# A local-attention and PReLU feed-forward kernel: the list that orders its first stage is rewritten, with maxima subtracted on VectorE and low parts formed in PSUM

## The chip, the cores and the metric

One core of one Trainium2 chip. The metric is device time in microseconds (us) of one execution; three executions of the kernel before took 771.10, 771.13 and 771.49 us, median 771.13.

## The reference, cut to what matters

```python
# q, k, v: (8, 8, 576, 64); sequence cut into chunks of 64; scale = 1/8
scores = scale * np.matmul(q_c, k_c.transpose(0, 1, 2, 4, 3))   # within a chunk
scores = scores - np.max(scores, axis=-1, keepdims=True)
attn = np.exp(scores)
attn = attn / (np.sum(attn, axis=-1, keepdims=True) + 1e-09)
out = np.matmul(attn, v_c)
x = out laid out as (4608 tokens, 512)
h = x @ w_in                                   # 512 x 2048
g = np.maximum(h, 0.0) + alpha * np.minimum(h, 0.0)
return g @ w_out                               # 2048 x 512
```

The weights arrive as 64-bit floats. The kernel turns each weight chunk into a 32-bit value and splits that into a high part and a low part in the matmul's input format; activations are split the same way, and each large product is made of three passes (high by high, low by high, high by low).

## The kernel before, in words

**Tiling.** The 4608 tokens are 36 sub-blocks of 128 tokens (two attention chunks each); four sub-blocks make a block of 512 tokens. The feed-forward's 2048 inner columns are 16 chunks `f` of 128. A first-layer step `h<b><f>` (line 422) is 12 matmuls of 128x512, an output step `o<b><f>` (line 458) is 12 more, into four PSUM tiles `t` of 128 tokens (two in the pair `ps_oa`, two in `ps_ob`). The first stage does the attention of sub-blocks 0 to 7, chunks 0 to 2 of block 0 and chunks 0 to 7 of block 1, and prepares weight chunks 0 to 8 of both matrices. Behind it come the rest of blocks 0 and 1, block 2, and pairs of blocks with a Strassen-like scheme whose weights are stored to DRAM by `keep_a` (line 597) and read back.

**What orders the first stage.** The string `START` (line 28) lists tokens; a loop (lines 931 to 932) issues them, and the order that results on PE, DVE, ACT, POOL and SP is kept as it stands. Each engine works through its own instructions in order. The tokens are:

- `q`, `k`, `v`: a load on SP's DMA queue (`q0`, `q1` on ACT's), lines 548 and 555; from 2 on, one load holds two sub-blocks. `W<n>`: n products of a zero tile, nothing reads them (line 898).
- `S<s>`: the 16 score products (line 261), into a PSUM bank pair. `m`: the row maxima, DVE (line 298). `z`, `e`, `a`, `r`, `n`: softmax (lines 299 to 325). For a sub-block in `SUBTRACTED`, `z` subtracts the maxima on DVE (302), `e` is one exponential on ACT (304), `a` a sum and an addition on DVE (307, 317). For the others, `z` scales the maxima on DVE (309), `e` is eight exponentials with accumulated sums, read straight from PSUM (313), `a` an addition on POOL (319). `r` is the reciprocal (321), `n` the multiplication (323), both on DVE.
- `T`: four transposes on PE (349). `p`: their copy to SBUF on ACT (356). `V`: 16 value products (367). `x`: the high part of x on ACT (373). `l`: the low part on DVE (375).
- `wi<f>`, `wo<f>` without a letter: the fetch of a raw weight chunk, 512 KB, on SP's queue (178). With a letter, the steps of its conversion: `b` absolute value on ACT (194), `k`, `h`, `u`, `v` bit work on DVE (196 to 202), `i` the high part on ACT (207), `j` the low part on DVE (209). `wi0` does `b` and `i` on DVE.
- `h`, `R`, `G`, `gh`, `gl`, `o`: the first layer on PE, its negative part on ACT (407), the PReLU on DVE (410), the high part on ACT (436), the low part on DVE (439), the output product on PE. `K<t>`: an output tile of block 0 is copied by ACT (492) and stored by a DMA on SP's queue (495).

**Buffers that make waits.** `BANKS` gives each S, T and V its PSUM pair: 0 is `ps_a`, 1 and 2 are `ps_oa` and `ps_ob`, which the output steps need from `o00` on. The tile `g` has two buffers, so `R` of one chunk waits for `gl` of the chunk two before. A `ps_h` bank (two of them) is free again after `G`. The 18 raw chunks of the list go round ten buffers (lines 169 to 177), so from the eleventh fetch on each waits for the conversion step `v` of the fetch ten before. `HALVES` names the scratch tile (`ta`, `tb`, `tc`) of each conversion. Outside the list, `keep_a` is issued by POOL once the last sub-block's low part is there (line 953) and the chunk is converted. Behind the list come `h18`, `o17` and, in an order that the framework's planner chooses, the next steps.

Of the kernel before, what the change touches and what calls it, by code (L numbers as in the profile page):

```python
# [10 lines left out]
F32 = mybir.dt.float32  # L11
# [8 lines left out]
def bits(pattern):  # L20
# [8 lines left out]
W8 q0 k0 k1 q1 q2 S0 W1 k2 m0 S1 W5 wi1 z0 m1 e0 wi0 z1 a0 e1 r0 S2 k4 n0 S3 m2 q4 wi1b z2 T0 W6 m3  # L29
e2 a1 z3 wi1k v0 wi0b r1 wi1h n1 wi2 p0 wi0k T1 a2 e3 wi0h r2 S4 W3 v2 wi0u n2 m4 q6 p1 V0 a3 z4  # L30
wi0v e4 T2 W4 k6 r3 wi0i wi1u wi0j wo4 wi1v x0 V1 n3 p2 wo0 l0 x1 V2 wi2b a4 l1 T3 x2 wo1 wi2k S5 p3
l2 wi1i V3 m5 v6 S6 r4 x3 z5 n4 e5 wi4 l3 h00 m6 v4 wi2h z6 wi1j e6 wi2u S7 wi3 a5 wi2v h01 m7 wo2
r5 R00 z7 n5 wo0b G00 wi5 wi2i T5 e7 wo0k wi2j h02 wi7 a6 wo0h r6 wo0u wo5 n6 p5 wo0v gh00 T6 wo1b
a7 T4 wo3 gl00 wo0i V5 r7 wo1k p6 wo0j x5 V6 n7 p4 l5 x6 T7 wo1h V4 l6 p7 wo1u x4 o00 R01 wo1v wo2b
G01 wo1i l4 gh01 wo1j R02 V7 gl01 o01 x7 wo2k G02 wi4b wi3b wo2h wo2u gh02 l7 h10 wo2v gl02 wo2i
wi3k wo2j wi4k wo4b o02 wi3h wi4h R10 wo4k wi4u K0 wi3u K1 G10 h11 wi4v gh10 wi3v wi4i gl10 K2 wi3i
wo4h wi4j K3 o10 wo4u wo5b wi3j R11 wo4v wi5b G11 wo4i wo6 h12 wo5k gh11 wo4j wi6 gl11 wo3b wo5h
wo3k wo5u wo8 o11 R12 wo3h wo5v wi8 G12 wo5i wo3u gh12 wo7 h13 wo5j gl12 wi7b wo3v wi5k wo3i wi7k
wi5h o12 R13 wo3j wi5u G13 wi5v gh13 h14 wi7h wi5i gl13 wi6b wi5j wi6k wi7u wi6h o13 R14 wi7v G14
wi7i wi6u gh14 wo6b wi6v h15 gl14 wi6i wo6k wi6j wi7j wo7b wo6h o14 wo7k R15 wo6u G15 wo6v gh15 wo7h  # L40
wi8b gl15 h16 wo6i wo7u wo7v wo6j wo7i wi8k o15 wo7j R16 wo8b G16 wi8h gh16 wi8u gl16 h17 wi8v wo8k
wi8i wi8j wo8h o16 R17 G17 wo8u gh17 wo8v gl17 wo8i wo8j
# [17 lines left out]
def tile_local_attention_prelu_ffn(  # L60
# [50 lines left out]
    def f32(t):  # L111
        return t.bitcast(F32)
# [181 lines left out]
    def early_softmax(s, sc3):  # L294

        mx = small.tile([P, H, 1], F32, name="mx", bufs=2)
# [3 lines left out]
        if s in SUBTRACTED:  # L300
# [59 lines left out]
    def early_values(s):  # L360
# [720 lines left out]
```

## Time and profile before

| what | value |
|---|---|
| median of three executions | 771.13 us (771.10 to 771.49) |
| span of the profiled execution | 770.2 us; no other time of that execution is given |
| PE, DVE, ACT, POOL busy | 760.4, 646.7, 447.3, 184.8 us |
| chain that ended last | PE 92%, ACT 4%, DVE 2%, DMA 2% |
| DMA | 184.5 MB, mean 240 GB/s |

The span runs from the first to the last instruction of the program in one profiled execution; the timed executions have a median 0.9 us above it. A busy share tells how much of the span an engine had something in work, not that it set the pace. The chain of waits is followed back from the last instruction, at each step to what released it. The timeline gives the start and the duration of each instruction (like ones in a row merged, xN), with the idle time of its engine ahead of it and who ended that; durations include the pipeline's tail, so start to start is often about 0.1 us shorter.

### The profile page before, as it was taken

What the parts mean: (1) busy time and instruction counts of PE and PEld (TensorE: products, weight loads), DVE (VectorE), ACT (ScalarE), POOL (GpSimd) and SP (SyncE); (2) the same over time, 40 slices, a digit from 0 to 9 for tenths busy, and PEclk for the clock granted to TensorE, in tenths of its full rate; (3) what the DMA queues carried; (4) which work ended last, traced back from release to release, by engine and by line L of the source; (5) the groups of instructions that cost most, each with busy time, mean ns of one, the idle gap of its engine ahead of it and who ended that gap; (6) DMA issues with size and microseconds to landing.
All of it is one profiled execution on the core that took longest, in us unless ns stands there. A gap on an engine that the chain in (4) does not pass through costs nothing.

```text
span 770.2 us, 15415 instructions
## 1 busy us (share of the span) xinstructions
PE 760.4 (99%) x5558; PEld 639.8 (83%) x5558; DVE 646.7 (84%) x1140; ACT 447.3 (58%) x1221; POOL 184.8 (24%) x304
## 2 busy tenths in 40 slices
PE   7999999999999999999999999999999999999998
PEld 7788887888888888888888888888888888888886
DVE  6999988989899886877899898777898977679784
ACT  6975555576666665666657456664574544354643
POOL 1153322343254331111121121111221121122110
PEclk9999999999999999999999999999999999999999
DMA  9859496468798775878765678875656765555573
GB/s 349 337 196 386 176 324 216 163 229 226 234 238 274 240 258 200 304 275 277 263 234 197 233 250 288 269 239 206 207 193 223 260 228 193 204 205 192 198 258 144
DMA packets 69322, 184.52 MB, mean 240 GB/s; under 512 B 10992, under 2 KB 18176, under 8 KB 69120
## 3 DMA queue, kind: packets, MB, share of 16 engines
q0 software_dynamic: 34336, 119.56, 45.9%
q1 hardware_dynamic: 34480, 63.20, 24.2%
q8 instruction: 44, 0.72, 0.4%
q10 hardware_dynamic: 432, 0.79, 0.3%
q14 instruction: 30, 0.25, 0.1%
HBM read 135.27 MB, written 42.99 MB: 231 GB/s over the span
## 4 chain that ended last, share of the span: by engine, by line
PE 92%; ACT 4%; DVE 2%; DMA 2%; issue 0%; ACTq 0%; SPq 0%
PE ps_o L722 20%; PE ps_o L850 19%; PE ps_h L422 14%; PE ps_h L722 10%; PE ps_h L850 10%; PE ps_oa L458 8%; PE ps_ob L458 7%; PE ps_a L388 2%; PE ps_a L272 2%; ACT wi L313 1%; ACT wo L313 1%; DMA raw<-w_in 1%; DMA raw<-w_out 1%; PE ps_h L898 1%; ACT wi L207 0%
## 5 line engine op out<-in xcount | busy, mean ns | idle before, releaser
L422 PE MATMUL ps_h<-xh,wi 128*128 128x512 f32 x384 | 101.7, 385 | 0.7 <-DVE g L410 0.5
L422 PEld LDWEIGHTS ps_h<-xh,wi 128*128 128x128 f32 x384 | 70.7, 187 | 13.8 <-DVE g L410 0.9
L722 PE MATMUL ps_o<-wi,raw 128*128 128x512 f32 x336 | 79.1, 382 | 0.0
L722 PEld LDWEIGHTS ps_o<-wi,raw 128*128 128x128 f32 x336 | 62.5, 187 | 11.2
L678 ACT CAST gh<-wo 128x512 fp32r<-128x512 f32 x66 | 41.0, 620 | 47.4 <-PE ps_o L850 31.8
L287 ACT ACTIVATE pr<-ps_a,mx 128x64 f32<-128x64 f32 x224 | 67.2, 325 | 0.8
L458 PE MATMUL ps_oa<-wo,gh 128*128 128x512 f32 x192 | 58.5, 385 | 0.1
L458 PE MATMUL ps_ob<-wo,gh 128*128 128x512 f32 x192 | 57.7, 380 | 0.0
L422 PE MATMUL ps_h<-xl,wi 128*128 128x512 f32 x192 | 50.6, 381 | 0.0
L679 DVE TENSOR_TENSOR gl<-wo,gh 128x512 fp32r<-128x512 f32 x63 | 43.2, 686 | 7.5 <-ACT gh L678 7.1
L287 ACT ACTIVATION_READ_ACCUMULATOR pr<-ps_a,mx 128x1 f32 x224 | 48.6, 217 | 0.0
L659 POOL DMA_DIRECT2D raw<-wi_a x42 | 22.3, 531 | 102.1 <-PE ps_o L722 54.5
L659 POOL DMA_DIRECT2D raw<-wo_a x42 | 22.2, 529 | 90.8 <-PE ps_o L850 51.2
L407 ACT ACTIVATE wo<-gh 128x512 f32<-128x512 f32 x24 | 15.2, 632 | 48.5 <-DVE gh L752 48.5
L678 ACT CAST ta<-wo 128x512 fp32r<-128x512 f32 x42 | 26.1, 621 | 26.4 <-PE ps_o L850 15.2
L422 PEld LDWEIGHTS ps_h<-xl,wi 128*128 128x128 f32 x192 | 35.8, 187 | 6.7 <-DVE xl L375 0.2
L458 PEld LDWEIGHTS ps_ob<-wo,gh 128*128 128x128 f32 x192 | 35.9, 187 | 6.4
L458 PEld LDWEIGHTS ps_oa<-wo,gh 128*128 128x128 f32 x192 | 35.3, 187 | 7.0 <-ACT gh L436 0.5
L722 PE MATMUL ps_o<-wi,wo 128*128 128x512 f32 x168 | 40.4, 383 | 0.0
L722 PE MATMUL ps_o<-wi,wi 128*128 128x512 f32 x168 | 40.4, 383 | 0.0
L722 PE MATMUL ps_h<-wi,raw 128*128 128x512 f32 x168 | 40.4, 382 | 0.0
L407 ACT ACTIVATE g<-ps_h 128x512 f32<-128x512 f32 x48 | 29.5, 614 | 17.5 <-PE ps_h L422 17.5
(296 smaller groups left out, 2036.2 us busy)
## 6 DMA issues: line engine op xcount, KB each, us to landing
raw<-wi_a POOLq DMA_DIRECT2D x42, 512.0 KB, 4.4
raw<-wo_a POOLq DMA_DIRECT2D x42, 512.0 KB, 3.5
wi<-wi_a POOLq DMA_DIRECT2D x21, 512.0 KB, 3.7
wo<-wi_a POOLq DMA_DIRECT2D x21, 512.0 KB, 4.3
wi<-wo_a POOLq DMA_DIRECT2D x21, 512.0 KB, 3.5
wo<-wo_a POOLq DMA_DIRECT2D x21, 512.0 KB, 3.6
k_sb<-kT SPq DMA_DIRECT2D x28, 256.0 KB, 4.7
q_sb<-qT SPq DMA_DIRECT2D x28, 256.0 KB, 4.1
```

Source lines behind the costliest of these rows:

```text
L272: pe(nc.tensor.matmul(att[0][c * C:(c + 1) * C, par, (NP + hp) * C:(NP + hp + 1) * C], lhsT=q_sb[rows, 2 * hp + c], rhs=kb[rows, 2 * hp + ...
L287: last = nc.scalar.activation(pr[:, g], sc3[:, g // NP, g % NP], AF.Exp, bias=mx[:, g], scale=SCALE, accum_out=sm[:, g])
L313: last = nc.scalar.activation(pr[:, g], sc3[:, g % 2, g // 2], AF.Exp, bias=mx[:, g], scale=SCALE, accum_out=sm[:, g])
L388: pe(nc.tensor.matmul(att[0][par * C:(par + 1) * C, c, hp * C:(hp + 1) * C], lhsT=v_sb[rows, h * C:(h + 1) * C], rhs=p[rows, :, par * NP + ...
L407: nc.scalar.activation(g, h, AF.Relu, scale=-1.0)
L422: pe(nc.tensor.matmul(woven(hps), lhsT=wi[f][:, l, k * P:(k + 1) * P], rhs=woven(xx[:, k]), start=(i == 0 and k == 0), stop=(i == 2 and k ...
L458: pe(nc.tensor.matmul(woven(o), lhsT=a[:, ts], rhs=woven(wo[f][:, l]), start=(f == first and i == 0), stop=(f == last and i == 2),))
L659: streamed[0] = nc.gpsimd.dma_start(out=f32(t), in_=units[side][n])
L678: hi = nc.scalar.copy(t_hi, t)
L679: return hi, nc.vector.tensor_tensor(t_lo, t, f32(t_hi), op=ALU.subtract)
L722: pe(nc.tensor.matmul(woven(ps), lhsT=w[:, l, k * P:(k + 1) * P], rhs=woven(xx[:, xl]), start=first and at == 0, stop=at == n - 1, skip_gr ...
L850: pe(nc.tensor.matmul(woven(ps[m]), lhsT=w[:, l, m * P:(m + 1) * P], rhs=woven(xx), start=i in (1, 5, 2) and j == 0 and n == 0, stop=j == ...
```

## The change

Sub-blocks 2 and 4 join sub-block 0 in subtracting the maxima on VectorE. For sub-blocks 1, 2 and 3 the low part of x is formed in PSUM: a new token `X` multiplies the high part by a negative identity (`minus`, made once on ACT) and adds it to the value products in their bank (two products of 128x256), and `l` is then a copy on ACT. The six runs of zero products (27 in all) go, and one of two, `W2`, comes ahead of `S2`. PSUM is given out by bank: a pair is one tile for the whole stage, transposes take one bank of a pair or a `ps_h` bank. `mx` and `sm` get a third buffer each. The list, the scratch names and the banks are rewritten.

```diff
@@ -26,32 +26,33 @@
 
 
 START = """
-W8 q0 k0 k1 q1 q2 S0 W1 k2 m0 S1 W5 wi1 z0 m1 e0 wi0 z1 a0 e1 r0 S2 k4 n0 S3 m2 q4 wi1b z2 T0 W6 m3
-e2 a1 z3 wi1k v0 wi0b r1 wi1h n1 wi2 p0 wi0k T1 a2 e3 wi0h r2 S4 W3 v2 wi0u n2 m4 q6 p1 V0 a3 z4
-wi0v e4 T2 W4 k6 r3 wi0i wi1u wi0j wo4 wi1v x0 V1 n3 p2 wo0 l0 x1 V2 wi2b a4 l1 T3 x2 wo1 wi2k S5 p3
-l2 wi1i V3 m5 v6 S6 r4 x3 z5 n4 e5 wi4 l3 h00 m6 v4 wi2h z6 wi1j e6 wi2u S7 wi3 a5 wi2v h01 m7 wo2
-r5 R00 z7 n5 wo0b G00 wi5 wi2i T5 e7 wo0k wi2j h02 wi7 a6 wo0h r6 wo0u wo5 n6 p5 wo0v gh00 T6 wo1b
-a7 T4 wo3 gl00 wo0i V5 r7 wo1k p6 wo0j x5 V6 n7 p4 l5 x6 T7 wo1h V4 l6 p7 wo1u x4 o00 R01 wo1v wo2b
-G01 wo1i l4 gh01 wo1j R02 V7 gl01 o01 x7 wo2k G02 wi4b wi3b wo2h wo2u gh02 l7 h10 wo2v gl02 wo2i
-wi3k wo2j wi4k wo4b o02 wi3h wi4h R10 wo4k wi4u K0 wi3u K1 G10 h11 wi4v gh10 wi3v wi4i gl10 K2 wi3i
-wo4h wi4j K3 o10 wo4u wo5b wi3j R11 wo4v wi5b G11 wo4i wo6 h12 wo5k gh11 wo4j wi6 gl11 wo3b wo5h
-wo3k wo5u wo8 o11 R12 wo3h wo5v wi8 G12 wo5i wo3u gh12 wo7 h13 wo5j gl12 wi7b wo3v wi5k wo3i wi7k
-wi5h o12 R13 wo3j wi5u G13 wi5v gh13 h14 wi7h wi5i gl13 wi6b wi5j wi6k wi7u wi6h o13 R14 wi7v G14
-wi7i wi6u gh14 wo6b wi6v h15 gl14 wi6i wo6k wi6j wi7j wo7b wo6h o14 wo7k R15 wo6u G15 wo6v gh15 wo7h
-wi8b gl15 h16 wo6i wo7u wo7v wo6j wo7i wi8k o15 wo7j R16 wo8b G16 wi8h gh16 wi8u gl16 h17 wi8v wo8k
-wi8i wi8j wo8h o16 R17 G17 wo8u gh17 wo8v gl17 wo8i wo8j
+k0 q0 q1 k1 S0 k2 S1 m0 z0 e0 W2 q2 wi1 m1 z1 a0 S2 r0 e1 wi0
+S3 n0 k4 m2 q4 a1 m3 T0 wi1b z2 r1 z3 v0 n1 v2 p0 e2 T1 a2 wi2
+wi0b S5 r2 wi0k e3 p1 a3 n2 T2 wi1k m5 r3 wo0 z5 wi1h S4 m4 wi0h p2 e5
+V0 z4 a5 V2 n3 wi0u T3 x0 q6 x2 k6 r5 p3 wi2b wi0v V1 x1 e4 l0 wo2
+n5 wi0i V3 X1 X2 x3 wi1u wi3 l1 wi0j X3 T5 l2 wi1v wi5 S6 l3 a4 S7 m6
+wo0b r4 v4 wo3 wi1i z6 p5 wi1j m7 wi2k n4 e6 a6 h00 h01 z7 wi6 wi2h wo0k T4
+r6 e7 wi2u n6 a7 wi2v wo0h T6 R00 r7 V5 p4 n7 wi2i G00 x5 wo0u wo2b v6 gh00
+wi2j V4 T7 x4 wo0v p6 wo0i l4 l5 h02 p7 V6 x6 wo0j gl00 wo1 wo1b V7 wi4 l6
+wo2k o00 wo1k wo7 R01 x7 G01 R02 gh01 l7 h10 wo1h wo2h wo1u G02 wo1v wo1i wo2u gh02 wo2v
+wo1j wi3b gl01 gl02 wi4b h11 wi4k wo2i wi3k wo2j wi4h R10 o01 G10 wi6b wi6k o02 wi4u gh10 wi3h
+gl10 wi3u K2 wi6h K0 wi3v K1 wi3i wi6u wo8 wi4v wi7 R11 G11 wi6v K3 wo4 wi4i wi6i wi3j
+wi4j h12 wi5b R12 wi6j wi5k G12 o10 wo3b h13 gh11 wi5h wo3k wi5u gh12 wo6 gl12 wo3h gl11 R13
+wo4b wi5v wo4k G13 wi5i h14 wo3u wo4h wi5j o11 wo3v R14 o12 wo4u wo4v wo6b h15 gh13 wo6k wo5
+wo4i wo3i G14 wo4j wi7b gl13 wo3j wo6h gh14 wi7k wo6u wo5b wo5k wo6v wo5h wi7h wo5u gl14 wo5v o13
+wo5i wi7u wi7v wo6i R15 wi7i wo6j h16 wo8b G15 o14 wo5j wi8 gh15 wi7j R16 h17 wo8k wo7b wi8b
+G16 wo8h gl15 gh16 wo7k wi8k wo8u wi8h wo7h gl16 R17 wo8v wo7u wi8u wo7v G17 wo8i wo7i o15 wi8v
+gh17 wo7j wi8i o16 gl17 wi8j wo8j
 """
 
 ALONE = ('wi0',)
-SUBTRACTED = (0,)
+SUBTRACTED = (0, 2, 4,)
+REMAINDERS = (1, 2, 3,)
 HALVES = {
-    "wi1": "ta", "wi0": "tb", "wi2": "tc", "wo0": "tb", "wo1": "ta", "wo2": "tc", "wi4": "tb", "wi3": "ta",
-    "wo4": "tc", "wo5": "tb", "wi5": "ta", "wo3": "tc", "wi7": "tb", "wi6": "tc", "wo6": "ta", "wo7": "tc",
-    "wi8": "tb", "wo8": "ta",
+    "wi0": "tb", "wi1": "ta", "wi2": "tc", "wi3": "tb", "wi4": "tc", "wi5": "tb", "wi6": "ta", "wi7": "ta", "wi8": "ta", "wo0": "tb", "wo1": "tc", "wo2": "ta", "wo3": "tc", "wo4": "ta", "wo5": "tc", "wo6": "tb", "wo7": "tc", "wo8": "tb",
 }
 BANKS = {
-    "S0": 1, "S1": 2, "S2": 0, "S3": 1, "T0": 2, "T1": 0, "S4": 2, "V0": 1, "T2": 0, "V1": 2, "V2": 0, "T3": 1,
-    "S5": 2, "V3": 1, "S6": 0, "S7": 1, "T5": 2, "T6": 1, "T4": 2, "V5": 0, "V6": 1, "T7": 2, "V4": 0, "V7": 0,
+    "S0": 4, "S1": 2, "S2": 4, "S3": 0, "S4": 0, "S5": 2, "S6": 2, "S7": 0, "T0": 2, "T1": 4, "T2": 7, "T3": 6, "T4": 4, "T5": 7, "T6": 0, "T7": 1, "V0": 4, "V1": 2, "V2": 0, "V3": 4, "V4": 4, "V5": 2, "V6": 4, "V7": 0,
 }
 LISTED = 18
 
@@ -147,10 +148,12 @@
     nc.vector.memset(table, 0.0)
     nc.scalar.activation(table, table, AF.Exp)
 
-    small.tile([P, 24], F32, name="rest")
+    small.tile([P, 8], F32, name="rest")
     gap.tile([P, 2 * SHIFT], F32, name="between")
     ident = small.tile([P, P], F32, name="ident")
     make_identity(nc, ident)
+    minus = room(FREE + RAWS + 1, [P, P], F32R)
+    nc.scalar.mul(minus, ident, -1.0)
     alpha_sb = small.tile([P, NF], F32, name="alpha_sb")
     rise = small.tile([P, NF], F32, name="rise")
 
@@ -240,9 +243,16 @@
             loads.append(nc.sync.dma_start(out=v_sb, in_=v[:, s]))
             qkv[s][2] = v_sb
 
+    pairs = {}
+
     def banks_of(token):
-        pool, name = ((ps_a, "ps_a"), (ps_o, "ps_oa"), (ps_o, "ps_ob"))[BANKS[token]]
-        return pool.tile([P, 2, TB], F32, name=name)
+        pair, bank = divmod(BANKS[token], 2)
+        if pair == 3:
+            return ps_h.tile([P, TB], F32, name="ps_h")
+        if pair not in pairs:
+            pool, name = ((ps_a, "ps_a"), (ps_o, "ps_oa"), (ps_o, "ps_ob"))[pair]
+            pairs[pair] = pool.tile([P, 2, TB], F32, name=name)
+        return pairs[pair][:, bank] if token[0] == "T" else pairs[pair]
 
     def quads():
         for hp in range(NP):
@@ -278,9 +288,9 @@
         return att[0][:, :, NP * C:].rearrange("p b (g k) -> p b g k", k=C)
 
     def attn_softmax(s, sc3):
-        mx = small.tile([P, H, 1], F32, name="mx", bufs=2)
+        mx = small.tile([P, H, 1], F32, name="mx", bufs=3)
         pr = soft.tile([P, H, C], F32, name="pr")
-        sm = small.tile([P, H, 1], F32, name="sm", bufs=2)
+        sm = small.tile([P, H, 1], F32, name="sm", bufs=3)
         scaled = nc.vector.tensor_reduce(mx.rearrange("p (b g) k -> p b (g k)", b=2), sc3, axis=AX.X, op=ALU.max)
         nc.scalar.mul(mx, mx, -SCALE)
         for g in range(H):
@@ -293,7 +303,7 @@
 
     def early_softmax(s, sc3):
 
-        mx = small.tile([P, H, 1], F32, name="mx", bufs=2)
+        mx = small.tile([P, H, 1], F32, name="mx", bufs=3)
         pr = prs[s // 2 % 2][:, s % 2]
         nc.vector.tensor_reduce(mx.rearrange("p (g c) k -> p c (g k)", c=2), sc3, axis=AX.X, op=ALU.max)
         yield
@@ -303,12 +313,12 @@
             yield
             last = nc.scalar.activation(pr, pr, AF.Exp, scale=SCALE)
             yield
-            sm = small.tile([P, H, 1], F32, name="sm", bufs=2)
+            sm = small.tile([P, H, 1], F32, name="sm", bufs=3)
             nc.vector.tensor_reduce(sm, pr, axis=AX.X, op=ALU.add)
         else:
             scaled = nc.vector.tensor_scalar(mx, mx, -SCALE, None, op0=ALU.mult)
             yield
-            sm = small.tile([P, H, 1], F32, name="sm", bufs=2)
+            sm = small.tile([P, H, 1], F32, name="sm", bufs=3)
             for g in range(H):
                 last = nc.scalar.activation(pr[:, g], sc3[:, g % 2, g // 2], AF.Exp, bias=mx[:, g], scale=SCALE, accum_out=sm[:, g])
             yield
@@ -344,7 +354,7 @@
     def early_transpose(s):
 
         pr = probs.pop(s)
-        tp = banks_of(f"T{s}")[:, 0]
+        tp = banks_of(f"T{s}")
         for hp in range(NP):
             pe(nc.tensor.transpose(
                 tp[:, hp * P:(hp + 1) * P],
@@ -365,14 +375,21 @@
         for hp, c, par, rows, to, cols in quads():
             h = 2 * hp + par
             pe(nc.tensor.matmul(
-                xo[to, c, cols], lhsT=v_sb[rows, h * C:(h + 1) * C], rhs=p[rows, h * C:(h + 1) * C], start=True, stop=True,
+                xo[to, c, cols], lhsT=v_sb[rows, h * C:(h + 1) * C], rhs=p[rows, h * C:(h + 1) * C],
+                start=hp == 0 or s not in REMAINDERS, stop=True, skip_group_check=hp > 0,
             ))
         yield
-        xo = by_chunk(xo)
+        banks, xo = xo, by_chunk(xo)
         xh, xl = (tokens(t, s) for t in x[s // SPB])
         nc.scalar.copy(xh, xo)
         yield
-        nc.vector.tensor_tensor(xl, xo, f32(xh), op=ALU.subtract)
+        if s in REMAINDERS:
+            for c in range(2):
+                pe(nc.tensor.matmul(banks[:, c, :NP * C], lhsT=minus, rhs=xh[:, c], start=False, stop=True, skip_group_check=True))
+            yield
+            nc.scalar.copy(xl, xo)
+        else:
+            nc.vector.tensor_tensor(xl, xo, f32(xh), op=ALU.subtract)
         yield
 
     def tokens(t, s):
@@ -908,7 +925,7 @@
         elif name == "V":
             running["values", s] = early_values(s)
             next(running["values", s])
-        elif name in ("x", "l"):
+        elif name in ("x", "X", "l"):
             next(running["values", s])
         elif name == "K":
             store(accs[0], 0, True, (s,))
```

## Rows read from the trace of the kernel before

**Rows 1.** The page: busy us of the engines (share of the span), instructions
```profile
PE 760.4 (99%) x5558; PEld 639.8 (83%) x5558; DVE 646.7 (84%) x1140; ACT 447.3 (58%) x1221; POOL 184.8 (24%) x304
```

**Rows 2.** Busy time by stretch: PE, PEld, DVE, ACT, POOL; clock; DMA share, GB/s
```profile
10.00:15.00 5.00, 2.73 (x28) 2.22 (x20) 4.77 (x14) 5.00 (x31) 0.64 (x2) 1.00 1.00 378
...
35.00:40.00 5.00, 4.40 (x94) 3.52 (x87) 4.97 (x9) 4.67 (x10) 0.00 (x0) 1.00 0.07 27
...
75.00:80.00 5.00, 5.00 (x25) 4.24 (x24) 4.97 (x10) 3.64 (x7) 2.02 (x4) 1.00 0.91 316
```

**Rows 3.** Chain that ended last, 0 to 85 us: start, us, what
```profile
44.22 2.64 PE ps_h L422 x12
46.86 1.32 PE ps_oa L458 x6
48.18 1.32 PE ps_ob L458 x6
...
81.18 2.64 PE ps_h L422 x12
```

**Rows 4.** Timeline, PE alone: start, us, instructions [idle before, ended by]
```profile
1.06 3.78 PE L898 MATMUL ps_h<-wo 128*128 128x128 f32 x16 [1.06 <-DVE table L147]
...
4.77 1.13 PE L261 MATMUL ps_oa<-wo,wo 64*64 64x64 f32 x32
...
8.95 0.69 PE L261 MATMUL ps_a<-wi,wi 64*64 64x64 f32 x32
...
11.64 1.50 PE L898 MATMUL ps_h<-wo 128*128 128x128 f32 x12
...
15.06 0.69 PE L261 MATMUL ps_ob<-wo,wo 64*64 64x64 f32 x32 [0.34 <-DMA wo<-qT]
...
20.72 0.69 PE L367 MATMUL ps_a<-wi,wi 64*64 64x64 f32 x32 [0.27 <-ACT wi L356]
21.34 0.66 PE L349 MATMUL ps_oa<-ident,wi 128*128 128x128 f32 x4
...
24.14 1.15 PE L422 MATMUL ps_h<-xh,wi 128*128 128x512 f32 x4 [0.24 <-ACT xh L373]
...
86.30 1.04 PE L422 MATMUL ps_h<-xh,wi 128*128 128x512 f32 x4
```

**Rows 5.** Groups by line, 0 to 90 us: xcount | busy us, mean ns
```profile
L898 PE MATMUL ps_h<-wo 128*128 128x128 f32 x54 | 9.5, 333 | 1.1 <-DVE table L147 1.1
L375 DVE TENSOR_TENSOR xl<-ps_a,xh 128x512 fp32r<-128x512 f32 x4 | 2.7, 685 | 0.0
L302 DVE TENSOR_TENSOR wo<-ps_oa,mx 128x512 f32<-128x512 f32 x1 | 0.7, 692 | 0.0
```

**Rows 6.** Timeline, ACT: the eight exponentials of sub-block 1 and what follows; two casts
```profile
8.60 0.31 ACT L313 ACTIVATE wo<-ps_ob,mx 128x64 f32<-128x64 f32 x1 [0.55 <-DVE mx L309]
...
10.93 0.71 ACT L194 ACTIVATE ta<-raw 128x512 f32<-128x512 f32 x1
...
20.52 0.63 ACT L373 CAST xh<-ps_ob 128x512 fp32r<-128x512 f32 x1
21.00 0.73 ACT L194 ACTIVATE tc<-more 128x512 f32<-128x512 f32 x1
```

**Rows 7.** Timeline, DMA issues: SP's partial stores and fetches, POOL's `keep_a`
```profile
48.83 0.33 SPq L495 DMA_DIRECT2D partial<-wo x1
...
52.88 2.89 POOL L597 DMA_DIRECT2D wi_a<-wi x4 [1.53 <-DVE wi L209]
```

**Rows 8.** DMA queues 53 to 64 us (packets, MB, share); issues at 48.83 and 57.60 (us to landing)
```profile
q0 software_dynamic: 591, 1.92, 54.2%
q1 hardware_dynamic: 685, 2.00, 46.8%
...
partial<-wo SPq DMA_DIRECT2D x1, 256.0 KB, 3.6
...
wo<-w_in SPq DMA_DIRECT2D x1, 512.0 KB, 9.8
```

## The prediction

> **What bounds the kernel now.** PE is busy 99% of the span [rows 1], so only what shortens or delays PE's own sequence can move the end. Next I read the stretches. From 10 to 15 us PE works 2.73 of 5 us while the DMA engines are full; from 75 to 80 it works all of it, and so does DVE, nearly (4.97) [rows 2]. The chain of waits says where PE becomes solid: from 44.22 us it is PE alone, 2.64 us for a first-layer step and 1.32 + 1.32 for an output step, up to `h17` at 81.18 [rows 3]. PE's timeline gives the marks: the first scores at 4.77, `S4` at 15.06 (it waits for the load of q), `h00` at 24.14, and `h18`, the first step behind the list, at 86.30 [rows 4]. So the change is worth what it does to that 86.30, plus what DVE owes at that point, since DVE is as full as PE and has no reserve to catch up with.
>
> The profiled execution has a span of 770.2 us; the median of the runs is 0.9 above it. I take that as constant and put my shifts on the median, 771.13. About 0.2% (1.5 us) is what a measurement of this kernel can tell from no change.
>
> **The parts on ACT, DVE and POOL.** Sub-blocks 2 and 4: eight exponentials hold ACT from 8.60 to 10.93, 2.33 us [rows 6]; one exponential holds it as long as a cast, 0.48 from start to start [rows 6]. ACT gains 2 x 1.85 = 3.7 us. DVE pays a subtraction and a sum for each, 0.69 apiece as line 302 [rows 5], so 2 x 1.38 = 2.8; the small additions moved from POOL replace the small scalings, zero net. Low parts of 1, 2 and 3: DVE gives back 3 x 0.685 = 2.05 [rows 5], ACT pays 3 x 0.48 = 1.4, PE pays six products of 256 columns at half of the 0.22 that a product of 512 takes (2.64 / 12, [rows 3]), some 0.7. Net: ACT -2.3, DVE +0.7, PE +0.7. The making of `minus`, third buffers, scratch names: nothing; ACT is idle until the first exponential. (If `minus` stood ahead of the issue of q1, `S1` would come 1.4 us later; the wait of `S4` for its load would swallow that.)
>
> **The zero products.** 54 records, 9.5 us of PE [rows 5], go but for four. They stand in waits, ahead of the load that `S4` waits for or of ACT, so they give PE little back. What they might buy is the clock. The stretches print a granted clock of 1.00 from the start [rows 2], yet the first 16 records take 3.78 us, 236 ns each, and twelve at 11.64 take 1.50, 125 each; `S0` takes 1.13 and `S2`, the same work, 0.69 [rows 4]. [...] In the changed kernel PE is idle until 4.8, and up to 15 us has only four scores, two transposes and `W2`, with gaps. A group at the lower level costs 0.44 more. Until 15 us the wait of `S4` hides that. If the clock stays low until 20, five groups pay 2.2, of which 1.0 fills waits counted below: +1.2; until 24, with four groups more, about +2.1. If it rises by 12: +0.1, and that I take, since `S2`, `S3` and the transpose behind them fill 3 us almost without a gap. [...]
>
> **PE's count up to the end of the list.** Before: 24.14 to 86.30 is 62.2 us, for 11 first-layer and 10 output steps (21 x 2.64 = 55.4), five score or value groups of 0.62 and four transpose groups of 0.60 (start to start, [rows 4]): 60.9, so 1.2 in waits and switches. After: the load for `S5` and `S4` has the same bytes ahead of it, so they start at 15.0. Then come, ahead of `h00`, eight groups of 0.62, three of 0.60 and 0.7 of new products: 7.5. Walking the queues with the durations above I find three waits: `V2` for the bank that sub-block 4's subtraction still reads, 1.2; `V3` for the bank until the low part of sub-block 0 is out, 0.9; the last new product for its cast, 0.4. That puts `h00` at 25.0. Behind it are 55.4, four groups of 0.62 and three of 0.60: 59.7, no wait over 0.1, and three breaks in the big products instead of six, so half of the 1.2: 85.3. **PE gains 1.0 us**, if nothing in 40 to 86 us comes late.
>
> **SP's queue, which the new list moves.** Fetches of `wo8`, `wi7` and `wo4` now stand behind the stores of `K2`, `K0`, `K1` (and `K3` ahead of `wo4`); SP issues in order, so buffers that are long free don't help. `K2` waits for the third tile of `o02`: 25.0 + seven big steps (18.5) + 4.3 of groups + 2.0 + 0.5 of switches = 50.3, its copy 0.6, so the store is issued at 50.9 (before: 48.83, [rows 7]). Up to the end of `wo4` ten units of 256 KB stand in that queue. A store issued alone landed after 3.6 us [rows 8]; the two queues together move 3.92 MB in 11 us, 0.356 MB per us [rows 8]. With the queue to itself `wo4` lands at 50.9 + 3.6 + nine units, 2.36 MB / 0.356 = 6.6: 61.1. But POOL's stores of weights run beside it: four were issued from 52.88 on [rows 7], and the new list converts `wi3`, `wi4` and `wi6` at that point, six units, up to 4.4 us more: 65.5. I take 63.6: between 53 and 64 us the queues shared almost evenly, 54% to 47% [rows 8], so more than half of the six come ahead. The row nearest in kind, a fetch at 57.60, took 9.8 us to land [rows 8].
>
> When is it wanted? `wo4`'s absolute value stands on ACT behind `R13`, which follows `h13` (PE: 50.9 + 3 x 2.64 = 58.9) and `gl11`: 60.2. Until the raw chunk lands, ACT stands still, with `wi5`'s cast, `R14`, `wo6` and `gh13` behind it; DVE stands at `wo4`'s next step, with `G13`, both `wo3` steps, `gl13` behind it. PE runs on until `o13`, due at 69.4, which needs `wo3`. From the absolute value to `wo3`'s low part DVE has some 8.0 us (13 instructions), so a landing by 61.4 costs nothing, and each us later is a us of PE: at 63.6, 2.2; at 65.5, 4.1; at 61.1, nothing. DVE ends the list as much later, and `wi8`, now converted last, is what `h18` needs: zero if the planner puts other products first, 1.5 at most, I take 0.7.
>
> **Sum:** -1.0 + 2.2 + 0.7 = +1.9, so **773.0 us**; ends of this case 771.5 and 775.0.
>
> **The rivals.**
> - **The fetch is in time** (by 61.4), clock high: PE's 1.0 stays, 770.1; with waits ahead of `h00` shorter than I walked them, down to 769.2. For it: with an otherwise empty queue 61.1 is enough. Against: fetches that took 9.8 us. This is the other side, decided by the landing of `wo4`.
> - **Late fetch and low clock** until 20 or later: 773.0 + 1.2 to 2.1, about 774.6. For it: the first 16 records' 236 ns. Against: `W2` and the scores leave no gap over 1.3 us from 4.8 to 11.
> - **They cancel:** fetch in time, clock low: 770.1 + 1.2 = 771.3.
>
> **How the numbers follow.** Chances: forecast 0.52, fetch in time 0.25, late and low 0.14, cancelling 0.09. Faster by over 0.2% (below 769.6) is half of the second: 0.13. Slower by over 0.2% (above 772.7) is seven tenths of the first, 0.36, and all of the third: 0.50. The rest, 0.37, is no change. The range 769.5 to 775.2 leaves out the fast end of the second case and the slow end of the third, under 0.2; both signs lie in it. The forecast's own range is 771.5 to 775.0.
>
> **What would show it.** Right: a wait of ACT near line 194 around 60 us that ends with a DMA, DVE idle for some 3 us beside it, a hole in PE at line 458 near 69 to 72, and `h00` near 25. Wrong: no such hole and `h18` near 85 (the fetch was in time); scores past 15 us that take 1.1 (clock); `h00` well off 25 (my walk of the banks).

## The result, and the profile after

The changed kernel takes **779.48 us** (median of four runs, 779.3 to 779.6); the kernel before took 771.31 beside it: ratio **1.0104, 95% interval 1.0091 to 1.0117**, slower by 8.2 us, outside the forecast range. The profiled execution has a span of 777.8 us and a time of 779.58.

From here on every list is cut at one place: the 4900th PE record from the end, counted in the trace. Before it lies the **front**, behind it the **rest**. The rest has the same number of products of the same shapes in every kernel (in some lists `o01` lies before the cut and `h10` behind it, in others the other way round; both are 12 products of 128x512). Front and rest are read from one profiled execution of each kernel. Before: 44.06 + 726.13 us. After: 42.85 + 734.93. So the front gained 1.2 us and the rest lost 8.8.

The page's line of busy times after (us, share of the span, instructions; before: [rows 1]), and PE's busy time by stretch behind 60 us in both kernels (PE, PEld, DVE, ACT, POOL; clock; DMA share, GB/s):

```profile
PE 759.5 (98%) x5514; PEld 637.1 (82%) x5514; DVE 646.2 (83%) x1141; ACT 444.4 (57%) x1195; POOL 183.8 (24%) x302
```

Before:

```profile
60.00:90.00 30.00, 30.00 (x138) 25.51 (x137) 28.88 (x56) 17.30 (x29) 10.09 (x13) 1.00 0.75 283
90.00:110.00 20.00, 20.00 (x92) 17.00 (x92) 17.47 (x32) 11.79 (x21) 4.42 (x6) 1.00 0.87 297
110.00:150.00 40.00, 39.50 (x235) 32.44 (x235) 37.20 (x71) 20.95 (x50) 13.33 (x19) 1.00 0.59 207
```

After:

```profile
60.00:90.00 30.00, 27.67 (x117) 22.73 (x116) 26.26 (x49) 15.18 (x27) 6.84 (x11) 0.94 0.73 260
90.00:110.00 20.00, 18.78 (x85) 15.29 (x84) 16.86 (x33) 10.98 (x20) 8.21 (x10) 1.00 0.69 227
110.00:150.00 40.00, 38.95 (x203) 31.95 (x202) 38.17 (x72) 21.74 (x49) 13.78 (x18) 1.00 0.76 272
150.00:200.00 50.00, 48.85 (x482) 40.59 (x482) 41.17 (x84) 29.82 (x108) 18.62 (x26) 1.00 0.67 197
```

Before, PE idles 0.5 us in the first three stretches; after, 2.33 + 1.22 + 1.05, and 1.15 more up to 200 us. In the first stretch the clock is down too (0.94). Where the first loss begins, four views of the kernel after say. SP's queue (start, us, what; before: [rows 7, 8]):

```profile
51.58 0.82 SPq L512 DMA_DIRECT2D partial<-wo  x2
52.98 0.33 SPq L181 DMA_DIRECT2D raw<-w_in  x1
53.41 0.41 SPq L512 DMA_DIRECT2D partial<-wi  x1
53.87 0.42 SPq L181 DMA_DIRECT2D more<-w_out  x1
54.34 0.48 SPq L181 DMA_DIRECT2D more<-w_in  x1
54.87 0.75 SPq L512 DMA_DIRECT2D partial<-wi  x1
55.66 0.43 SPq L181 DMA_DIRECT2D wo<-w_out  x1
```

The chain of waits, and ACT and DVE in the timeline:

```profile
55.66 8.39 DMA wo<-w_out
```
```profile
64.08 0.71 ACT L197 ACTIVATE ta<-wo 128x512 f32<-128x512 f32 x1 [3.78 <-DMA wo<-w_out]
...
64.82 0.43 DVE L199 TENSOR_SCALAR ta<-ta 128x512 f32<-128x512 f32 x1 [3.67 <-ACT ta L197]
```

PE in the timeline, at the head (before: [rows 4]) and at `o13`:

```profile
4.70 1.14 PE L271 MATMUL ps_ob<-wo,wo 64*64 64x64 f32 x32 [4.70 <-DMA wo<-qT]
...
17.62 0.89 PE L377 MATMUL ps_ob<-wo,wo 64*64 64x64 f32 x32
19.63 0.69 PE L377 MATMUL ps_a<-wi,wi 64*64 64x64 f32 x32 [1.13 <-issue]
...
22.21 0.69 PE L377 MATMUL ps_ob<-wi,wi 64*64 64x64 f32 x32 [0.67 <-ACT tc L197]
...
25.60 1.15 PE L439 MATMUL ps_h<-xh,wi 128*128 128x512 f32 x4
...
70.60 0.49 PE L475 MATMUL ps_oa<-wo,gh 128*128 128x512 f32 x1 [1.19 <-ACT wo L210]
72.23 0.49 PE L475 MATMUL ps_oa<-wo,gh 128*128 128x512 f32 x1 [1.14 <-DVE wo L212]
...
74.04 1.05 PE L475 MATMUL ps_ob<-wo,gh 128*128 128x512 f32 x2
...
101.86 0.72 PE L475 MATMUL ps_oa<-wo,gh 128*128 128x512 f32 x2 [1.07 <-ACT gh L453]
```

Busy time from 72.78 to 76.17 us (clock 0.50):

```profile
72.78:76.17 3.39, 3.39 (x9) 2.62 (x8) 3.39 (x8) 0.13 (x1) 0.42 (x1) 0.50 0.80 315
```

`wo4` is the eighth of a row of stores and fetches and lands at 64.06 (issued at 55.66, 8.39 on its way). ACT waits 3.78 us for it, DVE 3.67. PE is through with `h14` at 69.2, comes to `o13` and finds no `wo3`, whose conversion stands behind that of `wo4`. Then the granted clock is 0.50 until 76.2 us, 1.00 before and after: a pair of products takes 1.05 us where it took 0.60, and eight products from 72.78 on cost 0.21 us each more.

### The profile page after: what moved, and what is told of

Same layout as the page of the kernel before. It is cut to its first block, busy times and chain, and to the rows that moved or that the text cites. A ratio compares the mean times of both kernels' runs of the same rounds, so it can differ in the third digit from the quotient of the medians.

```text
span 777.8 us, 15307 instructions
## 1 busy us (share of the span) xinstructions
PE 759.5 (98%) x5514; PEld 637.1 (82%) x5514; DVE 646.2 (83%) x1141; ACT 444.4 (57%) x1195; POOL 183.8 (24%) x302
## 4 chain that ended last, share of the span: by engine, by line
PE 84%; DVE 6%; DMA 6%; ACT 2%; issue 1%; SPq 1%; ACTq 0%; DVEq 0%
PE ps_o L739 19%; PE ps_o L867 19%; PE ps_h L439 11%; PE ps_h L739 10%; PE ps_h L867 10%; PE ps_oa L475 5%; PE ps_ob L475 5%; PE ps_a L405 2%; DMA raw<-w_out 2%; PE ps_a L282 2%; DMA wo<-qT 1%; DMA wo<-w_out 1%; SPq L348 1%; DVE g L427 1%; DMA pT<-t 1%
## 5 line engine op out<-in xcount | busy, mean ns | idle before, releaser
L695 ACT CAST ta<-wo 128x512 fp32r<-128x512 f32 x42 | 26.1, 621 | 26.7 <-PE ps_o L867 15.5
```

Source lines behind the costliest of these rows:

```text
L695: hi = nc.scalar.copy(t_hi, t)
```

## The experiments

All times are medians; the kernel before took 771.0 to 771.5 in each set. `h00` is the start of the first first-layer step.

| run | us | ratio, 95% interval | h00 | front | rest |
|---|---|---|---|---|---|
| after | 779.48 | 1.0091 to 1.0117 | 25.60 | 42.85 | 734.93 |
| e1 fetches ahead of K2 | 775.21 | 1.004 to 1.007 | 26.94 | 44.14 | 729.93 |
| e2 `W8` at the head | 780.37 | 1.01 to 1.0133 | 26.36 | 43.56 | 735.07 |
| e3 both | 775.25 | 1.004 to 1.0069 | 26.89 | 44.13 | 729.26 |
| e4 before, zero products out | 774.97 | 1.0032 to 1.0066 | 26.76 | 47.68 | 725.49 |
| e5 fetches as converted | 774.72 | 1.0024 to 1.0048 | 25.88 | 43.14 | 729.25 |
| e6 zero products in waits | 783.25 | 1.0126 to 1.0165 | 28.57 | 45.79 | 735.69 |
| e7 = e5 + e6 | 777.46 | 1.0046 to 1.0106 | 28.22 | 45.44 | 730.91 |
| e8 = e7, lows on DVE | 776.14 | 1.0039 to 1.0079 | 25.25 | 43.97 | 730.40 |
| e9 new front, old back | 777.31 | 1.0067 to 1.0097 | 27.04 | 48.98 | 726.83 |
| e10 old front, new back | 776.02 | 1.0034 to 1.0076 | 24.23 | 44.20 | 730.04 |
| e11 = e7, wide zero products | 776.45 | 1.0055 to 1.0085 | 26.82 | 44.08 | 729.90 |
| e12 = e9 + wide zero products | 776.48 | 1.0057 to 1.009 | 26.84 | 47.70 | 726.43 |
| e13 old back from 48 us | 773.40 | 1.0019 to 1.004 | 25.80 | 43.01 | 727.86 |
| e14 old end from 72 us | 774.38 | 1.0025 to 1.005 | 26.74 | 43.94 | 727.81 |
| e15 before, maxima on DVE | 773.18 | 1.0013 to 1.0031 | 25.27 | 45.24 | 726.28 |
| e16 before, lows in PSUM | 775.85 | 1.0033 to 1.0067 | 25.62 | 46.91 | 726.36 |

**e1, e3: the fetches earlier.**

```diff
-gl10 wi3u K2 wi6h K0 wi3v K1 wi3i wi6u wo8 wi4v wi7 R11 G11 wi6v K3 wo4 wi4i
+gl10 wo8 wi7 wo4 wi3u K2 wi6h K0 wi3v K1 wi3i wi6u wi4v R11 G11 wi6v K3 wi4i
```

> Edit: the changed kernel with one thing moved, the fetches of wo8, wi7 and wo4 ahead of the store of K2 on SP's queue instead of between the stores. Theory (the late fetch is all of it): wo4 lands before 60 us, ACT's wait of 3.8 us ahead of its absolute value is gone, so are the holes of 1.2 and 1.1 us in PE at o13, the fall of the clock to 0.50 behind them at 72.8 to 76.2 us, and what came late behind the list; h18 within 1 us of 86.3 (it was at 90.5), time 770 to 772 us. First rival (the new list loads DVE and ACT too heavily whatever the fetches do): the hole closes, but h18 stays past 88 and the time at 775 or more. Second rival (the fetch costs only the hole at o13, and the stalls behind the list are their own): 775 to 777.

> Edit: both of the others, fetches of wo8, wi7 and wo4 ahead of the store of K2 and W8 back at the head. Theory (the two are independent, the fetch worth about 8 us, the clock at the start at most 1): 769.5 to 771.5 us, h18 at 85.5 to 86.5. If the early products gain more when no later wait swallows them, it is under 769.5 and beats the kernel before. Rival (a wait elsewhere takes the place of the hole): 773 or more.

The wait, the hole and the fall of the clock are gone (PE in e1, by stretch):

```profile
60.00:65.00 5.00, 5.00 (x24) 4.27 (x23) 5.00 (x11) 2.33 (x5) 2.10 (x3) 1.00 1.00 352
65.00:70.00 5.00, 5.00 (x24) 4.24 (x24) 4.96 (x10) 3.85 (x7) 2.18 (x4) 1.00 0.92 270
70.00:75.00 5.00, 5.00 (x25) 4.24 (x24) 4.98 (x11) 1.04 (x3) 0.72 (x1) 1.00 0.63 250
...
90.00:100.00 10.00, 8.25 (x37) 6.39 (x36) 6.88 (x13) 4.36 (x8) 4.01 (x6) 1.00 0.79 261
```

The rest falls by 5.0 us, and 3.8 remain: PE loses 1.75 of the ten us from 90 on. The theory (770 to 772) does not fit, and the first rival only in its time, as `h18` comes at 87.6 and not past 88; the second rival fits, at 775.21.

**e2, e4: the clock at the head.** e2 changes the changed list, e4 the kernel before (its other runs `W1`, `W5`, `W6`, `W3`, `W4` go too).

```diff
-k0 q0 q1 k1 S0
+W8 k0 q0 q1 k1 S0
```
```diff
-W8 q0 k0 k1 q1 q2 S0 W1 k2
+q0 k0 k1 q1 q2 S0 k2
...
-r0 S2
+r0 W2 S2
```

> Edit: the changed kernel with the first run of zero products, W8, back at the head of the list; nothing else. Theory: the scores from 4.8 us to 18 us go from about 1.1 us to 0.69, the granted clock shows from 7 us on, h00 moves from 25.6 to 25.0 or a little below, and the hole at o13 stays, since it hangs on the store of K2: 778.5 to 779.5 us, a gain of at most 1. Rival (the clock at the start is the cause): h00 at 24.2, most of the 8 us back, under 773.

> Edit: the kernel before without its zero products, but for W2 (four of its 54 records) ahead of S2 as in the change; nothing else is touched. Theory: the clock is low to about 18 us, groups ahead of 18 us take 1.1 instead of 0.69, h00 comes 0.5 to 1.2 us later than 24.14, and since PE has no reserve behind that, 771.5 to 772.5 us. Rival (the clock falls again at a later wait, because the zero products stood in the waits): above 773. Second rival (the waits for loads swallow it): 771.0 to 771.4.

e2:

```profile
10.00:15.00 5.00, 2.64 (x26) 1.71 (x20) 4.50 (x12) 4.33 (x24) 0.20 (x1) 0.50 1.02 414
15.00:20.00 5.00, 4.09 (x100) 3.46 (x100) 3.60 (x10) 3.66 (x22) 0.26 (x1) 0.57 1.02 418
```

e4:

```profile
15.00:20.00 5.00, 2.78 (x72) 2.13 (x66) 4.88 (x11) 5.00 (x33) 0.80 (x2) 0.57 1.02 416
20.00:25.00 5.00, 5.00 (x137) 4.38 (x133) 3.76 (x9) 3.53 (x8) 0.55 (x1) 0.50 1.03 417
25.00:30.00 5.00, 4.32 (x38) 3.55 (x37) 4.20 (x8) 4.78 (x30) 0.67 (x1) 0.56 1.03 419
```

In the new list a run at the head alone doesn't hold the clock: it is at 0.50 from 10 to 15 us, where PE waits for loads, and nothing is gained (e3 against e1 neither: 775.25 and 775.21). In the kernel before, the zero products, those at the head and those in the waits together, are worth 4.0 us (774.97 against 770.96): without them the clock lies low until past 25 us and `h00` comes at 26.76 instead of 24.14. Its first rival (above 773) was right.

**e5: which chunk each fetch takes.** The places are kept.

```diff
-wo2k o00 wo1k wo7 R01
+wo2k o00 wo1k wo4 R01
...
-wi6u wo8 wi4v wi7 R11 G11 wi6v K3 wo4 wi4i
+wi6u wo6 wi4v wi7 R11 G11 wi6v K3 wo7 wi4i
...
-gh12 wo6 gl12
+gh12 wo5 gl12
...
-wo6k wo5
+wo6k wo8
```

> Edit: the changed kernel, its fetches at the same places of the list, but each place takes a chunk in the order in which the list converts them: wo4 where wo7 stood, wo6 for wo8, wo7 for wo4, wo5 for wo6, wo8 for wo5. Theory (two effects of the fetch order: wo4 stands behind the stores, and the chunks that hold the four buffers raw, raw, more, more at the end of the list, wo7 and wo8 among them, are converted last, so the fetches behind the list wait): the hole at o13 goes as in the first experiment, and now also the stalls at 94 to 98, 128 and 134 us that were left there (2.1, 0.3 and 0.75 us); with h00 at 25.6 to 26.9 the time is 771 to 772.5 us. Rival (those stalls come from DVE's lack of time, not from the buffers): they stay, 775 us.

No hole, but the stalls from 93 us on stay, and with them the rival's 775: the order in which the buffers are filled is not what makes them. ACT and PE in the timeline of e5:

```profile
96.38 0.69 ACT L197 ACTIVATE tc<-raw 128x512 f32<-128x512 f32 x1 [2.60 <-DMA raw<-w_out]
96.97 0.59 ACT L424 ACTIVATE g<-ps_h 128x512 f32<-128x512 f32 x1
```
```profile
98.11 0.73 PE L475 MATMUL ps_oa<-wo,gh 128*128 128x512 f32 x2 [1.16 <-ACT gh L453]
```

The planner has put a conversion whose chunk is not there yet ahead of a first-layer step's negative part on ACT. That chunk was fetched at 91.06, when its buffer came free. In the kernel before, the fetch at the same place goes out later still (91.85) and PE has no such stall. There ACT has the negative part ahead of the conversion:

```profile
94.42 0.60 ACT L407 ACTIVATE g<-ps_h 128x512 f32<-128x512 f32 x1 [1.38 <-PE ps_h L422]
...
95.52 0.73 ACT L194 ACTIVATE tc<-raw 128x512 f32<-128x512 f32 x1
```

**e9, e10, e12, e14: front and back exchanged.** e9 follows the changed list up to `l7` and then the order of before; e10 is its mirror; e14 takes only the last steps, from `o13` on, from before; all fetch in the order of conversion. e12 is e9 with the zero products of e11, below. The lists at their joints:

```diff
-R02 gh01 l7 h10 wo1h wo2h wo1u G02 wo1v wo1i
+R02 gh01 l7 wi7 wo1h wo1u wo1v wo1i wo1j gl01 o01 G02
```
```diff
-gl14 wo5v o13 wo5i wi7u wi7v wo6i R15 wi7i wo6j h16 wo8b
+gl14 wo5v o13 wo5i wo5j wi7u wi7v wi7i wi7j wo7b o14 wo7k R15
```

> Edit: the changed kernel up to the last low part of the attention (token l7, some 46 us), and from there the rest of the steps in the order of the kernel before; each fetch takes the chunk that the list converts next. So the change's softmax, its low parts in PSUM, its banks and its missing zero products are in, its order of weights behind the attention is out. Theory (all that is lost behind 43 us comes from the order in which the new list converts and fetches the chunks at its back, its end included, where three conversions stand open and the planner then holds a first-layer step's PReLU behind other conversions): no hole at o13, no stalls at 94 to 101 us, at most 0.7 us of PE lost behind 66 us, h00 at 25.6 to 26.9, 769.5 to 771.5 us. Rival (the front is what makes the back late): stalls stay, 773 or more.

> Edit: the mirror of it: the kernel before, zero products and all, up to token l7, and from there the rest of the steps in the order of the changed list; each fetch takes the chunk that the list converts next, so wo4 isn't late. Theory (the back is at fault): the stalls of PE at 94 to 101, 128 to 136 us (some 2.5 us) show here too, with h00 at 24.1: 772.5 to 774.5 us. Rival (the back is harmless once the fetches are ordered): 770.5 to 771.5.

> Edit: the new front with the old back (the first of this set) plus the wide zero products of the third. Theory (the back no longer loses time, and the clock is up from 7 us on): h00 at 24.5 to 25.5, 768.5 to 770 us, under both kernels if the front's gain of about 1 us is real. Rival (PE's instruction blocks limit the front in any case): like the first of this set, within 0.5 us.

> Edit: the changed list up to its step o13 (some 72 us) with fetches in the order of conversion, and only the last steps in the order of the kernel before, so that one conversion stands open at the end of the list and not three. Theory (the end of the list decides what the planner does behind it): the stalls of PE at 94 to 101 us and 128 to 136 us go, the 4900 last products take 726 to 727.5 us instead of 729.3: 770.5 to 772.5 us. Rival (the chunks' order in the middle of the list, which sets the raw buffers, decides): the stalls stay, 774 to 775.

The rest sorts the runs by their backs: 725.5 to 726.8 with the old back from `l7` on or earlier, 729.3 to 730.9 with the new one and its fetches in time, 734.9 to 735.7 with `wo4` late; e13 and e14, which turn to the old order only at 48 and 72 us, lie between, at 727.9 and 727.8. So the back is at fault, whatever front it has; all five times of e10, 773.2 to 777.5, lie above the kernel before (770.5 to 771.9). e14, behind 90 us:

```profile
90.00:110.00 20.00, 20.00 (x92) 17.01 (x92) 18.39 (x35) 12.03 (x21) 6.27 (x8) 1.00 0.70 244
110.00:150.00 40.00, 39.90 (x210) 33.40 (x209) 38.56 (x74) 22.71 (x52) 12.07 (x17) 1.00 0.63 230
```

With the old end the stalls from 90 to 150 us go, so it is the last 12 us or so of the list that set what the planner does behind it. Only the profile shows this: the time of e14 is that of e5 (774.38 and 774.72), as its joint costs PE 1.5 us ahead of 90 us. The expected times are missed by e9, e12 and e14, as the joints make holes of their own: 2.46 us at `o01` in e9 and e12, whose `wo1` the splice converts too late, 1.42 us at 80 us in e14. In e9 the lower clock behind the hole (0.83 in the mean from 40 to 50 us) and a slow head (0.50 from 15 to 20 us, 0.60 to 25) come on top, and its front is 48.98. e10 lies 1.5 us above its own: its back costs 3.9 us (730.04 against 726.13).

**e13: a better joint.** e9 with the change of lists behind `G10`, some 48 us.

```diff
-R10 o01 G10 wi6b wi6k o02
+R10 o01 G10 wi7 wo4b o02
```

> Edit: the changed list up to its step G10 (some 48 us), then the rest in the order of the kernel before, fetches in the order of conversion. It is the new front with the old back again, but the switch comes behind the step o01, so that this step keeps the changed list's place and finds its weights converted. Theory (front 42.9 to 44.1 us up to the 4900th product from the end, back 726.1 to 726.8 as in every list with the old back): no hole at o01, no stalls behind 66 us beyond 1 us, 770 to 771.5 us, level with the kernel before and at its best 0.1% faster. Rival (the joint itself must cost, as DVE has less done at 48 us in the new list than the old back counts on): a hole between 48 and 70 us, 773 or more.

In its profile PE loses 1.3 us at the joint (50 to 55 us), 1.1 near 190 us, most of it in a wait for a load, and next to nothing between, and yet it is 773.40, not 770 to 771.5. Its profiled execution was the fastest of eight (span 770.9; the others 771.2 to 772.6). No version here beats the kernel before.

**e6, e7, e8, e11: zero products in the new front.** e6 is the changed list with them, e7 is e5 with them; e8 is e7 with `REMAINDERS = ()` and no `X`; e11 is e7 with products of 512 columns, 24 records instead of 66.

```diff
-k0 q0 q1 k1 S0 k2 S1 m0 z0 e0 W2 q2
+W8 k0 q0 q1 k1 S0 W1 k2 S1 m0 z0 e0 W5 q2
...
-e2 T1 a2 wi2 wi0b S5
+e2 W5 T1 a2 wi2 wi0b W4 S5
...
-V0 z4 a5 V2
+V0 z4 a5 W6 V2
...
-wi0i V3
+wi0i W4 V3
```
```diff
-                nc.tensor.matmul(hps[:, :P], lhsT=plain, rhs=plain, start=True, stop=True)
+                nc.tensor.matmul(hps, lhsT=plain[:, :P], rhs=plain, start=True, stop=True)
```

> Edit: the changed kernel with zero products back at the head (W8) and in PE's six waits ahead of h00 (W1, W5, W5, W4, W6, W4); fetches untouched. Theory (the clock stays at its upper level from 7 us on only if the waits are filled too, which W8 alone did not do): scores and transposes at 0.69 from 7 us on, granted clock 1.00 throughout 10 to 30 us, h00 at 24.2 to 24.8 (25.6 in the changed kernel), the hole at o13 stays: 777.5 to 779 us. Rival (the clock at the start costs nothing, loads bound the front): h00 stays at 25.6, no gain.

> Edit: both, fetches in the order of conversion and zero products at the head and in the waits. Theory (the list itself, maxima subtracted and low parts in PSUM, gains about 1 us in the front; all that the change lost is the fetch order and the clock): h00 at 24.2 to 24.8, no hole at o13, 769 to 770.5 us, level with the kernel before or up to 0.2% faster. Rival (DVE and ACT are worse off in the new list): 772 or more.

> Edit: the kernel of the run before this one with the low parts of sub-blocks 1, 2 and 3 on DVE again (no products with the negative identity, three subtractions of 0.69 us in their places). Theory: PE wins back 0.7 us of products and waits for casts, DVE pays 2.1 us and ACT wins 1.4; as DVE has little reserve ahead of the end of the list, within 1 us of that run, on either side. Rival (the low parts in PSUM are what makes the front shorter): 2 us slower than that run. Second rival (they only cost): 1 us or more faster.

> Edit: the kernel with ordered fetches and zero products in the waits (775 to 780 us), its zero products 512 columns wide instead of 128 and a third as many: 24 records instead of 66, some 5 us of PE either way. Theory (PE ran out of instructions in the middle of groups of small products, at its records 346 and 472, because a block of its instructions was still on its way; zero products bring PE to those places sooner and cost instructions of their own): with 42 fewer records the pauses of 1.0 to 1.8 us in the middle of groups of 32 at 20 to 28 us shrink to under 0.5 in sum or are gone, the clock stays up, h00 at 24.5 to 26: 772 to 773.5 us. Rival (the pauses belong to the place, a bank or a semaphore): they stay at V1 and S7, h00 at 28, 777.

The clock stays up (1.00, groups of 0.69 from 7 us on), but `h00` comes at 28.2 in e7 and 28.6 in e6, later than ever. PE in e7's timeline, and the queue of its instructions from 25.5 to 26 us:

```profile
20.34 0.50 PE L377 MATMUL ps_oa<-wo,wo 64*64 64x64 f32 x17
21.86 0.46 PE L377 MATMUL ps_oa<-wo,wo 64*64 64x64 f32 x15 [1.01 <-issue]
...
26.12 0.63 PE L271 MATMUL ps_a<-wi,wi 64*64 64x64 f32 x29
27.97 0.33 PE L271 MATMUL ps_a<-wi,wi 64*64 64x64 f32 x3 [1.21 <-issue]
```
```profile
q1 hardware_dynamic: 56, 0.20, 98.2%
q8 instruction: 1, 0.02, 11.4%
```

PE stops in the middle of a group, waiting for nothing that the profile shows. It does so after its 347th and its 473rd record in e6, e7 and e8 alike, though the 473rd lies in `S7` in e6 and e7 and in `h00` in e8. So the place is one of the instruction stream, not of a bank or a semaphore. The same pause stands in e4 and e10, 0.68 and 0.83 us after the 345th record, though e4 has four records of zero products and e10 has the front of the kernel before, which shows no such pause. In e11, with 42 records fewer, the pauses in groups are gone, as its theory said; but its wide products take PE time in the waits themselves (four of them 1.99 us from 18.64, two 1.13 from 22.39), `h00` is at 26.82, and the time (776.45) missed my 772 to 773.5. e8 against e7: 776.14 and 777.46, not told apart (in the profiles the front of e8 is 1.5 us shorter).

**e15, e16: each arithmetic part alone in the list of before.** 
```diff
-SUBTRACTED = (0,)
+SUBTRACTED = (0, 2, 4,)
```
```diff
-l1 T3 x2 wo1 wi2k S5 p3 l2
+X1 l1 T3 x2 wo1 wi2k S5 p3 X2 l2
...
-wi4 l3 h00
+wi4 X3 l3 h00
```

> Edit: the kernel before with sub-blocks 2 and 4 subtracting their maxima on VectorE as well, nothing else. Theory (a price as in the prediction's parts: ACT gains 3.7 us, DVE pays 2.8; between 10 and 25 us both are full, 4.7 to 5.0 of 5 us, and the maxima of the last sub-blocks stand on DVE behind it): h00 0 to 1.5 us later than 24.14, 771 to 773 us. Rival (ACT is what sets h00, so its relief shows): h00 at 23 to 23.5, under 770.5.

> Edit: the list of the kernel before in the changed code, with its own banks, one set of maxima subtracted on VectorE, its zero products, and the low parts of sub-blocks 1, 2 and 3 formed in PSUM, each product pair right ahead of its low part's copy. Theory (DVE gains 2.1 us ahead of h00, PE pays 0.7, ACT 1.4; DVE is what the kernel is short of up to the end of the list): between 1 us faster and 0.5 us slower, 770 to 771.5 us. Rival (the products stand in PE's queue waiting for casts, and ACT is as full as DVE): h00 0.7 to 2 us later, 772 to 773.

e15 is 1.1 us late at `h00` and nowhere else (rest 726.28). In e16 PE waits in the middle of `h00` for a low part that ACT now makes, and is 2.9 us late at the cut:

```profile
28.13 1.15 PE L443 MATMUL ps_h<-xl,wi 128*128 128x512 f32 x4 [1.46 <-ACT xl L394]
```

In both the granted clock is 0.66 from 15 to 20 us (before: 1.00). Neither part gains anything by itself.

## Why the prediction was wrong, step by step

- **The direction and the place were right.** The chain that it gave is the one in the trace: `wo4` behind the stores (forecast 63.6, landed 64.06), ACT's wait at line 194's operation (197 after) from 60.30, DVE idle, the hole at `o13`. The hole alone has the forecast's price: by its rule 64.06 - 61.4 = 2.7 us, and PE's starts show 1.35 + 1.41. The walk of the banks held too: `V2` and `V3` wait 1.13 and 0.67 us, forecast 1.2 and 0.9 (what ended the first, the profile does not name).
- **The term that failed first is the late fetch, sized 2.2.** With the fetches in order and nothing else moved (e5) the rest is 5.7 us shorter (734.93 against 729.25). In the medians of four pairs that differ in these fetches (after against e1 and against e5, e2 against e3, e6 against e7) it is worth 4.3 to 5.8 us. The step "each us later is a us of PE" left out what comes behind the hole: 8 x 0.21 = 1.7 us at the lower clock. Of the some 1.3 us that are left of the 5.7, about 1.1 are one wait for a load (`pT<-t`) at 198 us, 1.15 us in the kernel after. That wait can't be booked to the late fetch: it is 0.7 to 0.8 us in e9, e11 and e13, whose fetches are in time, and absent in e3 and e5. So the hole and the clock, some 4.5 us together, are what the profiles show of its cost; that DVE's idle 3.67 us cost anything more behind 90 us is not shown. That the landing came out so near was luck in part: the first store went out at 51.58 and not at 50.9, and the count had ten units of 256 KB in the queue, to which the planner added two, a fetch from `w_in` at 52.98.
- **The step from `wi8` to `h18`, sized 0.7, failed in kind.** The new back costs 3.1 us with fetches in time (729.25 against 726.13). It isn't `wi8` alone but the state in which the list ends, which sets the planner's order for the next 50 us (e10, e14). The prediction read the list up to its last token and costed what lies behind by one wait.
- **PE's count: -1.0 forecast, -1.2 measured** (42.85 against 44.06), but with `h00` at 25.60, forecast 25.0: it comes 0.6 late, and that the gain still has the forecast's size is luck. The pace rises at 18 us, not by 12: groups take 1.09 to 1.14 until 17.6 us, 0.60 to 0.69 from 19.63 on, and the trace's first record of the clock, 1.00, begins at 18.16. `S2`, `S3` and the transpose, from 8.56 to 11.88 us with one gap of 0.24, still take 1.14, 1.11 and 1.09. The sentence on a clock low until 20 us gave +1.2; a part of that fell into waits. All zero products of the kernel before together are worth 4.0 us (e4), more than the 2.1 that the prediction allowed; the run at the start alone shows no gain in the new list (e2: 780.37 against 779.48). The gain of the front hangs on a thread: lists with the same head have `h00` at 25.6 to 25.9 (after, e5, e13) or at 26.7 to 27.0 (e1, e9, e14), the clock rising at 18 to 19 or at 24 us, and with the latter nothing of it is left.
- **The net on ACT and DVE (-2.3 and +0.7), which the sum left at nothing,** was taken too lightly: alone in the old list, the maxima on DVE cost 0.22% and the low parts in PSUM 0.5% (e15, e16).
- Added: -1.2 + 5.7 + 3.1 = 7.6 us, the difference of the two profiled spans (777.8 - 770.2). The medians differ by 8.2: a time lies some 1.8 us above its span in nearly all runs, so the profiled execution of before took, by estimate, about 772.0, 0.7 above the median of 771.31. The 0.9 that the prediction took for a constant was these 1.8 less the 0.9 by which that execution was slower than 771.13.

What stays open: which of the last steps makes the planner's order worse, and why one and the same head of the list runs at two speeds.

## What to carry to other kernels

Price a hole in the bottleneck's work by what follows it as well: here the lower clock behind it added 1.7 us to a hole of 2.8. A list written by hand hands its end state to whatever plans the steps behind it, so cost that joint too, by the conversions that stand open there. Put fetches into the queue in the order of their use, ahead of stores that wait for results: here that was worth 4.3 to 5.8 us.

## What the runs showed of the hardware

The runs speak for PE's instructions coming in blocks for which PE can have to wait: the pauses of e6, e7 and e8 are 1.00 to 1.76 us long. 126 records lie between the two of each run, 6.1 to 6.7 us apart, with the DMA share at 1.02 to 1.03; 32 small products take 0.5 us (25.61 to 26.12 in e7), so 126 of them are done sooner than that. The trace shows one packet of 16 KB on the instruction queue ahead of each pause, at 19.35 and 25.66 us in e7. In all eight pauses (two each in e6, e7 and e8, one each in e4 and e10) PE goes on 2.25 to 2.54 us after the start of that packet. That the pause is the wait for the block is an inference from the record numbers and these times; no row names it. So zero products that keep the clock up also spend instructions: in the old front 54 records pass without a pause in the kernel before and with one of 0.83 us in e10, in the new one 66 cost more than the clock gives (783.25 us against 779.48, 777.46 against 774.72).

Behind the hole at `o13` (two pauses of PE, 1.19 and 1.14 us) the products took twice their time for 3.4 us (a pair 0.85 us from start to start where it took 0.44), at a granted clock of 0.50. In e9 they did so behind its hole of 2.46 us (pair 0.85), and in e6 behind one of 2.55 (clock 0.72 in the mean from 70 to 75 us); in e12, with the same hole as e9 at the same step, they kept their pace (clock 1.00), as they did behind single pauses of 1.0 to 1.5 us beyond 60 us (e5, e10, e14; clock 1.00). So the length of a hole alone does not tell what it costs.
